# Attention times V by full-array products over two heads, in a sliding-window attention with a mixture of adapters

## The chip, the cores and the metric

One NeuronCore of a Trainium2 chip runs the whole program. The metric is the device time of one execution in microseconds. The engines are called PE (matrix products; PEld is its loading of weights), DVE (VectorE), ACT (ScalarE), POOL (GpSimd) and SP (SyncE). Each of them works through its own instructions in order and waits on semaphores for the others. Loads of q, k and v are issued from POOL's queue, stores of the output and loads of the adapters' weights from SP's.

## What is computed

There are 8 batches of 8 heads, 576 positions and 64 elements per head, all in float32. Attention is limited to a window of 32 positions to each side. Its output, with the heads side by side, is the input x (4608 rows of 512) of a mixture of 8 adapters of rank 16, of which each row takes the best two.

```python
scores = scale * np.matmul(q, k.transpose(0, 1, 3, 2))
mask = np.abs(pos[:, None] - pos[None, :]) <= window          # window = 32
attn = softmax(np.where(mask, scores, -1e9))
x = np.matmul(attn, v)            # then (B, H, S, D) -> (B * S, H * D)
logits = x @ w_gate;  topk = the two largest;  w = softmax over these two
delta = sum over the two of w * ((x @ A[e]) @ B[e])
return x + delta
```

## The kernel before

The 64 heads are taken in pairs. A pair's keys are cut into 9 blocks of 64 positions, and a block together with the queries that its window reaches is a slot; 8 slots make a score tile T, of which there are 36. For four steps n in a batch b there is one product with V, numbered u = 4b + n, so 32 of them.

The order of the work is written out by hand, as the string ORDER (lines 51 to 101): a list of words such as `PV.2:2`, each of which calls the function of that name, with its numbers; what follows the colon is the bank of PSUM (0 to 2 for the wide tiles W, 3 and 4 for the narrow tiles T) or the engine (A for ACT, D for DVE, P for POOL). The program keeps that order on each engine and on each queue. The words, in the order in which data passes through them:

- LD (line 166) loads 128 rows of q or k, LV (line 178) a batch's v in rows of two positions. With each row of v the two positions lie side by side, so SV (line 185) moves every second one to 32 other partitions. LV and SV of v are numbered by the half o of the partitions; there are 17 LV and 32 SV, 29 of these on POOL and 3 on DVE. Five v tiles take turns (NV, line 41); Z1 (line 505) sets their column of ones once.
- TR (line 194) turns q or k by 16 transposes on PE, EQ and EK (lines 204 and 214) copy them out of PSUM.
- SM (line 226) puts the mask into a score tile, by four products that each use a quarter of the PE array (64 rows, 64 columns) and write 512 columns. SC (line 239) adds the scores in 16 quarter products, EX (line 244) takes the exponential into a tile PT, whose borders ZP (lines 508 and 509) has cleared once.
- PV (line 262) multiplies PT by v. Head one of the pair lies in partitions 0 to 63 and head two in 64 to 127, both of PT and of v. Each of 13 steps is a pair of products, one for each half of the rows of the array, that write 65 columns each (a sum and 64 outputs) into different banks. So a PV has 26 matmuls.
- MU (lines 275 and 280) divides by the sums into x, one reciprocal and one product of 640 columns on DVE.
- TX, XE, PZ (lines 307, 313, 323) turn x and multiply it by the adapters' A and the gate; G1a, G1b, GA and G2 (lines 349 to 375) make the gates on DVE and ACT; TZ and ZE turn the result.
- PD (lines 420 and 424) multiplies by B. Where OB, which brings the output out of PSUM, is on ACT (line 447), PE also adds x, by four more matmuls (line 424); where OB is on DVE (line 449), DVE adds x. ST (line 455) stores.
- WM (line 501) does products of zeros and CM, MM, MC (lines 476 to 494) make the mask.

Of the kernel before, what the change touches and what calls it, by code (L numbers as in the profile page):

```python
# [29 lines left out]
QW = NR * FT + 8  # L30
GS = 188
VD = D + 1
V0 = 8
VW = 136
GV = 66
NS = NP * NB
NEG = -30000.0
NU = B * NP
NV, NPT, NRAW, NX, NXT, NOB = 5, 6, 5, 3, 3, 12
NW, NT = 3, 2  # L40
LB = B - 1

# [6 lines left out]


ORDER = """
CI Z1.0 CQ LD.0.0 Z1.3 ZP.5 LD.0.1 ZP.2 LD.1.0 ZP.0 LV.0.1 ZP.4 LD.1.1 LD.2.0 TR.0.0:3 CM
TR.0.1:4 EQ.0:A LD.2.1 WM.2.4:0 EK.0:D LD.3.0 ZP.1 MM:4 MC Z1.1 SM.1:0 LV.1.1 TR.1.0:4 TR.1.1:3
LD.3.1 EQ.1:D SM.0:1 EK.1:A LD.4.0 Z1.2 ZP.3 TR.2.0:4 SM.2:2 EQ.2:D SC.0 SV.0.1.1:P TR.2.1:3
EX.0 Z1.4 WM.0.4:4 EK.2:D LV.0.0 SC.2 LD.4.1 SC.1 EX.2 SM.3:1 SC.3 TR.3.0:3 LD.5.0 EX.1
TR.3.1:4 EQ.3:A SM.4:0 EX.3 WM.1.4:3 SV.1.1.0:P EK.3:A LD.5.1 SC.4 LD.6.0 SM.5:1 SV.0.0.0:D EX.4
TR.4.0:4 PV.2:2 LV.1.0 EQ.4:A PV.3:0 SC.5 SV.0.0.1:P MU.3 EX.5 TR.4.1:4 MU.2 LV.2.1 PV.1:0
EK.4:A SV.1.1.1:P PV.0:1 MU.1 SM.7:2 LD.6.1 MU.0 SM.8:0 SC.8 SC.7 TR.5.1:4 LD.7.0 EX.7 TR.5.0:3
LD.7.1 EK.5:D SM.6:1 EQ.5:A SC.6 LD.8.0 WG LV.2.0 WA EX.8 TX.0.1:4 LD.8.1 SM.9:2 EX.6 TR.6.0:3
SV.1.0.0:P SV.1.0.1:D TX.0.0:0 EQ.6:A SC.9 XE.0.0:D PV.5:1 EX.9 SV.2.1.0:P MU.5 PV.4:0 MU.4  # L60
SV.2.1.1:P SM.10:2 TR.7.0:3 XE.0.1:D PV.6:1 LV.3.1 MU.6 TR.6.1:4 LD.9.0 TX.0.2:0 EK.6:A LD.9.1
XE.0.2:D SM.11:1 PV.7:0 EQ.7:A TR.7.1:4 MU.7 SC.10 TR.8.0:3 EX.10 EK.7:D SC.11 SM.12:0
SV.2.0.1:P EX.11 EQ.8:D TX.1.0:4 WD:D LD.10.0 SC.12 SM.13:1 WC:D EX.12 SC.13 LD.10.1 PV.8:2
SV.2.0.0:P TR.8.1:3 EX.13 XE.1.0:D PZ.0:0 MU.8 LD.11.0 EK.8:A TX.1.2:4 G1a.0 SM.14:1 XE.1.2:A
LV.3.0 PV.9:2 G1b.0 GA.0 TX.1.1:3 SV.3.1.0:P MU.9 SC.14 TR.9.0:4 EX.14 XE.1.1:D LV.4.1 PV.11:2
G2.0 EQ.9:A SV.3.1.1:P TR.9.1:3 TR.10.0:1 EK.9:A LD.11.1 MU.11 PV.10:0 TZ.0:4 LD.12.0 EQ.10:D
TR.10.1:3 ZE.0:A LV.4.0 SM.17:2 MU.10 SC.17 TR.11.0:4 LD.12.1 EX.17 PD.0.3:1 EQ.11:D PZ.1:0
EK.10:A OB.0.3:D TX.2.1:4 G1a.1 TX.2.2:3 SV.3.0.0:P XE.2.1:A TX.2.0:1 XE.2.2:D PD.0.1:2 XE.2.0:D
PD.0.0:3 LD.13.0 OB.0.1:A PD.0.4:4 PD.0.2:1 OB.0.0:A OB.0.4:D SM.18:2 OB.0.2:A LV.5.1 SC.18
G1b.1 TR.11.1:3 GA.1 ST.0.2.2 EX.18 SV.4.1.0:P PZ.2:1 G2.1 ST.0.1.1 EK.11:A SV.3.0.1:P SM.15:2  # L70
SC.15 G1a.2 TZ.1:4 EX.15 SV.4.1.1:P G1b.2 SM.16:0 SC.16 ZE.1:D TR.12.0:3 GA.2 EX.16 LD.13.1 G2.2
PV.12:2 TR.12.1:4 EQ.12:A LV.5.0 SM.19:0 SC.19 MU.12 EK.12:A PV.14:1 SV.4.0.1:P PD.1.3:3 MU.14
# [12 lines left out]
OB.3.4:D TX.5.2:4 TX.5.1:1 G1a.4 XE.5.2:A PD.3.1:3 G1b.4 GA.4 TX.5.0:0 OB.3.1:A XE.5.1:D
TR.17.0:4 XE.5.0:A TR.16.0:3 EQ.17:D SM.27:1 EQ.16:A SC.27 G2.4 PZ.5:0 EX.27 TR.16.1:3
SV.7.1.0:P G1a.5 PD.3.0:4 G1b.5 EK.16:A TZ.4:1 SM.29:2 ZE.4:D SC.29 GA.5 OB.3.0:D EX.29 SM.30:1
PD.4.2:3 G2.5 SC.30 OB.4.2:A SM.31:2 SC.31 EX.30 PD.4.4:4 PD.4.0:3 OB.4.4:D PV.26:0 OB.4.0:A
PV.24:1 ST.4.4.24 MU.26 EX.31 PD.4.3:4 ST.3.1.16 ST.3.0.15 TR.17.1:3 MU.24 ST.4.0.20 OB.4.3:A
SV.7.0.0:P PV.27:2 ST.3.4.19 EK.17:A ST.4.2.22 PV.25:0 MU.27 TZ.5:4 SV.7.0.1:P SM.33:1 ZE.5:A  # L90
SC.33 MU.25 SM.32:2 EX.33 SV.7.1.1:P SC.32 PD.4.1:4 SV.8.1.0:D PD.5.1:3 SM.35:0 EX.32 OB.4.1:D
SM.34:1 SC.35 SC.34 OB.5.1:D ST.4.1.21 TX.6.0:4 EX.35 ST.3.2.17 PV.28:2 XE.6.0:D TX.6.1:3 EX.34
MU.28 PV.30:0 TX.6.2:4 XE.6.1:A PV.31:1 MU.30 PV.29:2 XE.6.2:A PD.5.0:3 MA.31 PZ.6:0 OB.5.0:A
MU.29 ST.5.0.25 PD.5.2:3 ST.4.3.23 MB.31 TX.7.0:4 G1a.6 OB.5.2:A TX.7.4:1 TX.7.2:2 G1b.6 GA.6
ST.5.2.27 TX.7.1:3 XE.7.0:A XE.7.4:D XE.7.1:A G2.6 PD.5.3:4 PD.5.4:1 XE.7.2:A TX.7.3:3 XE.7.3:A
PZa.7:2 OB.5.4:A OB.5.3:D TZ.6:3 PZb.7 ZE.6:D ST.5.4.29 ST.5.1.26 G1a.7 PD.6.0:3 ST.5.3.28 G1b.7
GA.7 PD.6.1:4 OB.6.0:A PD.6.2:1 G2a.7 OB.6.1:A ST.6.0.30 PD.6.4:3 OB.6.2:A PX.7.2:0 ST.6.1.31
OB.6.4:A G2b.7 TZa.7:4 PX.7.4:1 ZEa.7:A TZb.7:2 ST.6.4.34 PX.7.3:3 ZEb.7:A ST.6.2.32 PB.7.2
PX.7.1:4 OB.7.2:A PB.7.3 PB.7.1 OB.7.3:D PX.7.0:2 OB.7.1:A PB.7.4 ST.7.2.99 PB.7.0 PD.6.3:0
OB.7.4:A OB.7.0:D ST.7.3.99 ST.7.1.99 OB.6.3:A ST.7.4.99 ST.7.0.99 ST.6.3.33  # L100
"""


# [1 line left out]
def kernel(  # L105
# [62 lines left out]
            f += n  # L168

    def LV(b, o):
        h0 = 8 * b + (2, -2)[o]
        skip = 2 if h0 < 0 else 0
        n = min(h0 + 4, B * H) - h0 - skip
        src = v.rearrange("b h s d -> (b h) s d")[h0 + skip:h0 + skip + n]
        src = src.rearrange("n (a p two) d -> p (n a) (two d)", p=32, two=2)
        keep(nc.gpsimd.dma_start(  # L178
            out=vs[b % NV][64 * o:64 * o + 32, NB * skip:NB * (skip + n), V0:V0 + 2 * D], in_=src))


    def SV(b, o, h):
        d = vs[b % NV][:, NS // 2 * h:NS // 2 * h + NS // 2]
        p0 = 64 * o
        keep(copy_on("SV", b, o, h)(out=d[p0 + 32:p0 + 64, :, V0:V0 + D],  # L185
                                    in_=d[p0:p0 + 32, :, V0 + D:V0 + 2 * D]))


    def TR(t, w):
# [29 lines left out]

    QUARTERS = [(e, o, 64 * (o ^ e ^ 1)) for e in (0, 1) for o in (0, 1)]  # L220

    def SM(T):
        p = ps("SM", T).rearrange("p (i c) -> p i c", c=128)
        for e, o, r0 in QUARTERS:
            c0 = 64 * o
            keep(nc.tensor.matmul(  # L226
                out=p[r0:r0 + 64, 4 * e:4 * e + 4], lhsT=twice[c0:c0 + 64, 0:64],
                rhs=bcast(maskK[c0:c0 + 64], 1, 4), start=True, stop=False,
                tile_position=(c0, r0)))


    def SC(T):
# [17 lines left out]
    def PV(u):  # L250
        b, n = divmod(u, NP)
        po = ps("PV", u)
        for g in range(NG):
            ops = [(a, off) for a, off in ((2 * g - 1, 128), (2 * g, 64), (2 * g + 1, 0))
                   if 0 <= a < NB]
            for i, (a, off) in enumerate(ops):
                T, sl = divmod(NB * (2 * b + n % 2) + a, TB // 2)
                sl += TB // 2 * (n // 2)
                for o in (0, 1):
                    r = slice(64 * o, 64 * o + 64)  # L260
                    c0 = 512 * (o ^ (n < 2)) + GV * g
                    keep(nc.tensor.matmul(  # L262
                        out=po[:, c0:c0 + VD], lhsT=PTs[T % NPT][r, sl, off:off + 128],
                        rhs=vs[(b + (o and n // 2)) % NV][r, NB * (n ^ 2) + a, V0 - 1:V0 + D], start=(i == 0),
                        stop=(i == len(ops) - 1), tile_position=(64 * o, 0)))

    rcs = {}

    def sums(u):
        p = ps("PV", u).rearrange("p (h c) -> p h c", h=2)[:, :, 0:GV * NG]  # L270
        return p.rearrange("p h (g c) -> p g h c", c=GV)

    def recip(u):
        rcs[u] = small.tile([128, NG, 2], F32, tag="rc", name="rc")
        keep(nc.vector.reciprocal(out=rcs[u], in_=sums(u)[:, :, :, 0]))  # L275

    def mult(u, g0, g1):
        b, n = divmod(u, NP)
        xg = xs[b % NX].rearrange("p g (h n d) -> p g h n d", h=2, n=NP)
        keep(nc.vector.tensor_tensor(out=xg[:, g0:g1, :, n], in0=sums(u)[:, g0:g1, :, 1:VD],  # L280
                                     in1=bcast(rcs[u][:, g0:g1], 3, D), op=ALU.mult))

    def MU(u):
        recip(u)
# [217 lines left out]
                                  start=True, stop=True))  # L502

    def Z1(i):
        keep(nc.vector.memset(vs[i][:, :, V0 - 1:V0], 1.0))

    def ZP(i):
        keep(nc.vector.memset(PTs[i][:, :, 0:64], 0.0))
# [62 lines left out]
```

## Time and profile before

| | |
|---|---|
| three timed runs, us | 144.29, 144.80, 145.91 (median 144.8) |
| the profiled execution, us | 143.44, of which the span of its instructions is 141.6 |
| granted PE clock, mean | 0.964 |
| loads and stores | 28.85 MB read, 9.44 MB written |
| POOL's last load of v issued at, us | 83.2 |
| POOL's DMA issues of q, k and v | 24, 24 and 17 |

In the page, a group's row gives busy time, the mean of one in ns, then the idle time of the engine just before them and what ended it. In the windows view each row is a stretch of the span, with busy time and the number of instructions of each engine, the granted clock, the DMA share and GB/s. In the chain of waits, which follows the work that ended last back to the start, each row is a start, a duration and what filled it; "issue" is time in which an engine waited for nothing that the profile shows.

### The profile page before, as it was taken

Reading aid. Unit: us, or ns where it says so; the run is one execution under the profiler, and the core shown is the slowest. Engines: PE = TensorE matmul, PEld = TensorE weight load, DVE = VectorE, ACT = ScalarE, POOL = GpSimd, SP = SyncE. Lnnn points to the kernel's source line nnn. Section 1 sums busy time; section 2 is a strip of 40 time slices with the busy share of each in tenths; the row PEclk is TensorE's granted clock in tenths of the full one; section 3 lists DMA queues with packets and bytes.
Section 4 is the critical chain, followed back from the end, with each engine's and each line's share of the span. In section 5 each row is a group of like instructions: output and inputs, shape, how many; then the busy total and the mean of one; then the engine's idle time right before and its main releaser. Section 6 shows DMA issues by size and latency. Waiting matters only on the chain.

```text
span 141.6 us, 5983 instructions
## 1 busy us (share of the span) xinstructions
PE 113.2 (80%) x2637; PEld 85.5 (60%) x2637; DVE 96.5 (68%) x235; ACT 86.8 (61%) x116; POOL 78.7 (56%) x103
## 2 busy tenths in 40 slices
PE   0389977729595995899875999859999998999950
PEld 0237636627473784797753477647887775878830
DVE  7165306550856869977984599898889798997430
ACT  3113789175253748379871568575878889565850
POOL 7999879998099999999995773630000000000000
PEclk9999999995999599999998699999999999999999
DMA  0999999999999999999999399291660095153885
GB/s 0 188 195 199 199 191 203 184 203 184 224 199 202 187 192 172 176 147 174 192 226 189 50 155 233 71 304 49 227 192 0 5 283 197 47 199 110 282 315 172
DMA packets 35288, 24.50 MB, mean 173 GB/s; under 512 B 21312, under 2 KB 30528, under 8 KB 35264
## 3 DMA queue, kind: packets, MB, share of 16 engines
q0 software_dynamic: 28688, 14.16, 76.1%
q1 hardware_dynamic: 6576, 9.98, 21.5%
q8 instruction: 20, 0.33, 1.0%
q14 instruction: 4, 0.03, 0.1%
HBM read 28.85 MB, written 9.44 MB: 270 GB/s over the span
## 4 chain that ended last, share of the span: by engine, by line
PE 60%; DVE 17%; issue 10%; ACT 5%; DMA 3%; POOL 1%; DVEq 0%; POOLq 0%; ACTq 0%
PE W L262 9%; PE T L194 9%; PE W L226 7%; PE T L420 6%; PE W L239 6%; PE T L424 5%; PE W L323 5%; PE T L307 4%; DMA l<-in_k_dram 3%; DVE zs L375 3%; PE W L307 3%; ACT PT L244 2%; PE W L424 2%; DVE gate L367 2%; DVE x L280 2%
## 5 line engine op out<-in xcount | busy, mean ns | idle before, releaser
L244 ACT ACTIVATE PT<-W 128x1024 f16<-128x1024 f32 x36 | 36.3, 1027 | 16.0 <-PE W L239 12.7
L185 POOL COPY v<-v 32x1152 f16<-32x1152 f16 x29 | 33.5, 1160 | 13.0 <-DMA v<-in_v_dram 12.3
L194 PE MATMUL T<-ident,l 128*64 128x128 f16 x528 | 22.9, 235 | 10.1 <-DMA l<-in_q_dram 5.6
L194 PEld LDWEIGHTS <-l 128*64 128x64 f16 x576 | 19.3, 118 | 16.9 <-issue 8.3
L280 DVE TENSOR_TENSOR x<-W,rc 128x640 f16<-128x640 f32 (+2 forms) x33 | 26.5, 804 | 1.1
L262 PE MATMUL W<-v,PT 64*128 64x65 f16 x832 | 18.1, 193 | 4.8 <-issue 3.7
L214 ACT COPY kR<-T 128x1024 f16<-128x1024 f16 x14 | 14.2, 1016 | 9.4 <-PE T L194 9.3
L226 PE MATMUL W<-maskK,twice 64*64 64x512 f16 x144 | 16.1, 433 | 3.2 <-DVE zs L375 1.7
L262 PEld LDWEIGHTS <-PT 64*128 64x128 f16 x832 | 14.8, 96 | 6.2 <-issue 4.0
L239 PE MATMUL W<-qR,kR 64*64 64x128 f16 x576 | 15.8, 231 | 3.0 <-issue 2.5
L239 PEld LDWEIGHTS <-kR 64*64 64x64 f16 x576 | 12.4, 114 | 7.8 <-issue 5.1
L166 POOL DMA_DIRECT2D l<-in_q_dram x24 | 15.8, 661 | 0.9 <-DMA l<-in_q_dram 0.5
L166 POOL DMA_DIRECT2D l<-in_k_dram x24 | 15.6, 652 | 0.0
L204 ACT COPY qR<-T 128x1024 f16<-128x1024 f16 x10 | 10.2, 1015 | 5.8 <-PE T L194 5.8
L178 POOL DMA_DIRECT2D v<-in_v_dram x17 | 13.7, 806 | 0.0
L275 DVE RECIPROCAL rc<-W 128x10 f32<-128x10 f32 x32 | 6.9, 216 | 8.6 <-PE W L262 8.6
L447 ACT COPY ob<-T 128x512 f32<-128x512 f32 x14 | 8.2, 588 | 6.6 <-PE T L424 4.7
L424 PEld LDWEIGHTS <-xT 128*128 128x128 f16 x96 | 10.1, 121 | 3.2
L420 PE MATMUL T<-B_sb,zT 128*128 128x512 f16 x30 | 11.6, 410 | 0.4 <-ACT xT L313 0.2
L307 PEld LDWEIGHTS <-x 128*128 128x128 f16 x160 | 10.7, 118 | 1.4 <-issue 0.4
L323 PE MATMUL W<-WA_sb,xT 128*128 128x136 f16 x160 | 11.0, 223 | 0.0
L449 DVE TENSOR_TENSOR ob<-T,x 128x512 f32<-128x512 f32 x14 | 9.4, 685 | 2.0 <-PE T L420 1.8
(76 smaller groups left out, 148.3 us busy)
## 6 DMA issues: line engine op xcount, KB each, us to landing
out_dram<-ob SPq DMA_DIRECT2D x24, 256.0 KB, 2.8
v<-in_v_dram POOLq DMA_DIRECT2D x15, 288.0 KB, 7.6
l<-in_q_dram POOLq DMA_DIRECT2D x12, 256.0 KB, 6.5
l<-in_k_dram POOLq DMA_DIRECT2D x12, 256.0 KB, 7.1
out_dram<-ob SPq DMA_DIRECT2D x16, 192.0 KB, 2.7
l<-in_q_dram POOLq DMA_DIRECT2D x4, 192.0 KB, 6.7
l<-in_k_dram POOLq DMA_DIRECT2D x4, 192.0 KB, 5.7
l<-in_q_dram POOLq DMA_DIRECT2D x4, 128.0 KB, 7.4
```

The lines of the kernel that those rows point to most:

```text
L166: keep(nc.gpsimd.dma_start(out=raw[w][t % NRAW][f - FT * t:f - FT * t + n], in_=src[f - NF * b:f - NF * b + n]))
L185: keep(copy_on("SV", b, o, h)(out=d[p0 + 32:p0 + 64, :, V0:V0 + D], in_=d[p0:p0 + 32, :, V0 + D:V0 + 2 * D]))
L194: keep(nc.tensor.matmul(out=tp[64 * o:64 * o + 64, FT * slot:FT * slot + FT], lhsT=raw[w][t % NRAW][:, o, D * j:D * j + D], rhs=ident, is_ ...
L226: keep(nc.tensor.matmul(out=p[r0:r0 + 64, 4 * e:4 * e + 4], lhsT=twice[c0:c0 + 64, 0:64], rhs=bcast(maskK[c0:c0 + 64], 1, 4), start=True, ...
L239: keep(nc.tensor.matmul(out=p[r0:r0 + 64, 4 * e + i], lhsT=kR[r, a], rhs=qR[r, :, 8 * a:8 * a + 16], start=False, stop=(i == TB // 2 - 1), ...
L244: keep(nc.scalar.activation(out=PTs[T % NPT][:, :, 64:192].rearrange("p i (f j) -> p i f j", j=J), in_=ps("SM", T).rearrange("p (i j f) -> ...
L262: keep(nc.tensor.matmul(out=po[:, c0:c0 + VD], lhsT=PTs[T % NPT][r, sl, off:off + 128], rhs=vs[(b + (o and n // 2)) % NV][r, NB * (n ^ 2) ...
L280: keep(nc.vector.tensor_tensor(out=xg[:, g0:g1, :, n], in0=sums(u)[:, g0:g1, :, 1:VD], in1=bcast(rcs[u][:, g0:g1], 3, D), op=ALU.mult))
L307: keep(nc.tensor.matmul(out=tp[:, c0:c0 + 128], lhsT=fourth(xs[b % NX][:, g], c), rhs=ident, is_transpose=True, start=True, stop=True))
L323: keep(nc.tensor.matmul(out=pz(b)[:, GS * g:GS * g + ER + E], lhsT=xTs[b % NXT][:, g, c, :], rhs=WA_sb[:, c, :], start=(c == 0), stop=(c = ...
L420: keep(nc.tensor.matmul(out=pd, lhsT=zTs[b % 2][:, g], rhs=B_sb, **kw))
L424: keep(nc.tensor.matmul(out=fourth(pd, c), lhsT=xTs[b % NXT][:, g, c], rhs=ident, start=(first and c == 0), stop=(not first and c == 3)))
```

## The change

Five things are changed together.

1. PV no longer uses two half arrays. The v tile gets 194 columns instead of 136, so that each partition has room for both heads: partitions 0 to 63 hold head one in columns 0 to 64 (its ones first) and zeros in columns 129 to 193, partitions 64 to 127 hold head two in columns 129 to 193 (its ones last) and zeros in columns 0 to 64. A step of PV is one product with all 128 rows and 130 columns, 13 instead of 26 in a PV.
2. The zeros are written once, by the new word ZV, eight times 64 partitions of 36 x 65 elements, six on DVE and two on ACT. There are four v tiles instead of five. Z1 sets its ones in two pieces.
3. LV takes three loads for a batch instead of two that straddle batches (24 instead of 17, the same bytes), and v starts at an odd element of the tile. Of the 32 SV, 19 are on POOL and 13 on DVE.
4. MU takes the two heads in two products of 320 columns each where they have to be swapped (n of 0 and 1).
5. SM's mask is two products of half the rows and all columns, instead of four quarters.

ORDER is new as a whole. On PE it holds the same 233 steps. OB is on DVE 22 times instead of 18 (on ACT 18 instead of 22), and WD and WC, which convert the adapters' weights, are on ACT instead of DVE. One group of zero products (WM.2.4) stands at the end of PE's list instead of near the start.

```diff
-V0 = 8
-VW = 136
-GV = 66
+VW = 3 * D + 2
+V1 = VW - VD
+GV = 171
-NV, NPT, NRAW, NX, NXT, NOB = 5, 6, 5, 3, 3, 12
+NV, NPT, NRAW, NX, NXT, NOB = 4, 6, 5, 3, 3, 12
...
+    def LV(b, i):
+        h0, n, s0 = ((2, 4, 0), (6, 2, 0), (0, 2, 2))[i]
+        p0, c0 = (96, VD) if i else (0, 1)
+        src = v[b, h0:h0 + n].rearrange("n (a p two) d -> p (n a) (two d)", p=32, two=2)
         keep(nc.gpsimd.dma_start(
+            out=vs[b % NV][p0:p0 + 32, NB * s0:NB * (s0 + n), c0:c0 + 2 * D], in_=src))
...
     def SM(T):
         p = ps("SM", T).rearrange("p (i c) -> p i c", c=128)
-        for e, o, r0 in QUARTERS:
-            c0 = 64 * o
-            keep(nc.tensor.matmul(
-                out=p[r0:r0 + 64, 4 * e:4 * e + 4], lhsT=twice[c0:c0 + 64, 0:64],
-                rhs=bcast(maskK[c0:c0 + 64], 1, 4), start=True, stop=False,
-                tile_position=(c0, r0)))
+        for h in (0, 1):
+            r = slice(64 * h, 64 * h + 64)
+            keep(nc.tensor.matmul(out=p[:, 4 * h:4 * h + 4], lhsT=twice[r], rhs=bcast(maskK[r], 1, 4),
+                                  start=True, stop=False, tile_position=(64 * h, 0)))
...
-                for o in (0, 1):
-                    r = slice(64 * o, 64 * o + 64)
-                    c0 = 512 * (o ^ (n < 2)) + GV * g
-                    keep(nc.tensor.matmul(
-                        out=po[:, c0:c0 + VD], lhsT=PTs[T % NPT][r, sl, off:off + 128],
-                        rhs=vs[(b + (o and n // 2)) % NV][r, NB * (n ^ 2) + a, V0 - 1:V0 + D], start=(i == 0),
-                        stop=(i == len(ops) - 1), tile_position=(64 * o, 0)))
+                vv = vs[b % NV][:, NB * (n ^ 2) + a, 0:VD]
+                vv = dataclasses.replace(vv, ap=[list(vv.ap[0]), [V1, 2], [1, VD]])
+                keep(nc.tensor.matmul(
+                    out=po[:, GV * g:GV * g + 2 * VD], lhsT=PTs[T % NPT][:, sl, off:off + 128],
+                    rhs=vv, start=(i == 0), stop=(i == len(ops) - 1)))
...
+        U = sums(u, g0, g1)[:, :, 1:1 + 2 * D].rearrange("p g (h d) -> p g h d", h=2)
+        if n < 2:
+            for h in (0, 1):
+                keep(nc.vector.tensor_tensor(
+                    out=xg[:, g0:g1, 1 - h, n], in0=U[:, :, h],
+                    in1=bcast(rcs[u][:, g0:g1, h], 2, D), op=ALU.mult))
...
+    def ZV(i, o):
+        d = vs[i][64:128, :, 0:VD] if o else vs[i][0:64, :, V1:VW]
+        if where["ZV", i, o] == "A":
+            keep(nc.scalar.copy(out=d, in_=bcast(zero[64 * o:64 * o + 64, 0:VD], 1, NS)))
+        else:
+            keep(nc.vector.memset(d, 0.0))
```

129 lines of the change are left out of this document (63 added, 66 removed).

## The prediction

> **What bounds the kernel now.** I read the page first: busy times, slices, shares of the chain.
>
> ```profile
> PE 113.2 (80%) x2637; PEld 85.5 (60%) x2637; DVE 96.5 (68%) x235; ACT 86.8 (61%) x116; POOL 78.7 (56%) x103
> ...
> PEclk9999999995999599999998699999999999999999
> DMA  0999999999999999999999399291660095153885
> ...
> PE 60%; DVE 17%; issue 10%; ACT 5%; DMA 3%; POOL 1%; DVEq 0%; POOLq 0%; ACTq 0%
> ```
>
> PE carries 60% of the chain, and another 10% (14 us) is "issue". The DMA engines are full until about 78 us, yet DMA has only 3% of the chain: loads run ahead. So the question is what PE does all day, and what stops it. The view of PE's waits answers the second half (total, times, longest):
>
> ```profile
> PE W L262 <- issue: 3.7, 3, 2.0
> PE T L194 <- issue: 2.9, 2, 1.6
> PE W L239 <- issue: 2.5, 1, 2.5
> PE W L226 <- DVE zs L375: 1.7, 1, 1.7
> PE W L194 <- issue: 1.4, 1, 1.4
> ```
>
> Seven stops with no visible cause hold 10.5 us, on three unrelated lines; waits for other engines are small beside them. I then cut windows from the end of one stop to the end of the next. Columns: stretch, length, busy us and count for PE, PEld, DVE, ACT, POOL, then granted clock, DMA share, GB/s.
>
> ```profile
> 25.24:31.70 6.46, 3.52 (x128) 2.72 (x128) 4.12 (x9) 2.99 (x4) 6.36 (x9) 1.00 1.50 195
> 31.70:39.01 7.31, 5.79 (x127) 4.18 (x127) 3.16 (x6) 3.06 (x3) 3.27 (x5) 0.77 1.38 204
> 39.01:45.05 6.04, 4.14 (x128) 3.22 (x127) 3.68 (x7) 2.95 (x3) 6.00 (x8) 1.00 1.36 201
> 56.62:75.88 19.26, 15.91 (x382) 12.75 (x383) 15.09 (x39) 12.95 (x17) 19.09 (x23) 1.00 1.33 183
> 75.88:119.93 44.05, 41.01 (x1020) 30.48 (x1020) 37.88 (x84) 32.62 (x43) 9.94 (x11) 0.96 0.64 147
> 32.50:35.80 3.30, 3.30 (x51) 2.20 (x50) 0.46 (x1) 1.66 (x2) 2.44 (x4) 0.50 1.43 178
> 46.10:49.50 3.40, 3.40 (x80) 2.69 (x80) 3.04 (x10) 2.73 (x3) 3.40 (x5) 0.50 1.68 187
> 76.90:80.10 3.20, 3.20 (x52) 1.40 (x46) 2.36 (x5) 1.43 (x3) 1.27 (x2) 0.50 0.73 116
> 0.00:21.70 21.70, 14.23 (x262) 8.69 (x263) 8.94 (x27) 9.78 (x11) 19.18 (x34) 1.00 1.13 163
> ```
>
> The stops stand 128 matmuls and 128 weight loads apart, or a multiple of it (383 is three times, 1020 eight times, give or take a lost record). So instructions come to PE in blocks of 256, and while DMA is full a block needs 6.0 to 7.3 us from the end of one stop to the end of the next. PE runs its 256 in 3.5 to 4.1 us in two of these windows and then stands. The three rows at clock 0.50 follow the long stops before 31.70, 45.05 and 75.88 within 1.1 us: a stop also costs a stretch of half clock.
>
> So PE bounds the kernel almost from the start, partly by its own work, partly by the number of its instructions. The change moves these two against each other.
>
> **PE's own work.** The chain gives the pace of products, where PE waits for nothing:
>
> ```profile
> 21.77 0.93 PE W L262 x52
> ...
> 101.01 0.51 PE W L262 x26
> 101.52 0.32 PE T L420
> 101.84 1.18 PE W L323 x20
> ...
> 111.97 0.44 PE T L424 x4
> 112.41 0.91 PE W L262 x52
> ```
>
> A PV after other work takes 0.51, a second right behind it 0.91 - 0.51 = 0.40 (31 ns for a pair of 65 columns: the halves run side by side). After the change a step is one full-array matmul of 130 columns. The nearest row is L323's, full array and 136 columns: 1.18 / 20 = 59 ns. Scaled by columns it is 56.4; I take 57, bounds 56 and 59. A PV is then 13 x 57 = 0.74 us, 0.34 more; 32 of them: **+10.9** (bounds +10.5 and +11.8). The zeros are paid in full.
>
> The 0.11 between 0.51 and 0.40 is the price of changing how the array is divided. Counted in the two orders, such changes go from 124 to 119: **-0.5**.
>
> OB moves to DVE four times, and with it PE's four matmuls of 0.44 (L424) go: **-1.8**. SM halves its matmuls; its 512 columns pass in the same time if the two halves run side by side, as PV's did: 0. If they didn't, it would be 512 columns at 57 / 130 ns each, 0.22 us, times 36, +8; PV's 31 ns per pair speaks against it. PE's work: **+8.6**.
>
> **The start.** DVE gets six clears of 36 x 65 = 2340 elements, and all stand before the first PV. Rows by shape:
>
> ```profile
> L280 DVE TENSOR_TENSOR x<-W,rc 128x640 f16<-128x640 f32 x31 | 25.6, 825 | 1.1
> L449 DVE TENSOR_TENSOR ob<-T,x 128x512 f32<-128x512 f32 x14 | 9.4, 685 | 2.0 <-PE T L420 1.8
> ...
> L214 DVE COPY kR<-T 128x1024 f16<-128x1024 f16 x4 | 4.9, 1222 | 5.0 <-PE T L194 5.0
> L204 DVE COPY qR<-T 128x1024 f16<-128x1024 f16 x5 | 3.5, 693 | 3.5 <-PE T L194 3.4
> ...
> L185 DVE COPY v<-v 32x1152 f16<-32x1152 f16 x3 | 1.8, 589 | 5.2 <-DMA v<-in_v_dram 5.1
> L508 DVE MEMSET PT<- 128x256 uint32 x6 | 1.6, 272 | 0.0
> ...
> L505 DVE MEMSET v<- 128x36 f16 x5 | 0.4, 88 | 0.4
> L280 DVE TENSOR_TENSOR x<-W,rc 128x256 f16<-128x256 f32 x1 | 0.4, 415 | 0.0
> ```
>
> A clear of 256 words takes 272 ns, 1.06 each, so 2340 take 2.49 us; two f16 to a step would halve it to 1.24, and L505's rate (88 / 36) would make 5.7. Its 88 ns are mostly a fixed part, so I take 2.45. The Trainium skill, "VectorE: DVE Perf Modes", section "Zero memsets can be issued as uint32 (trn2)", says that a memset takes one cycle per element whatever the type, and that only a whole number of 4-byte words can be issued as uint32; rows of 65 f16 are none. By its 0.96 GHz that is an estimated 2.44 us; no run here shows it yet.
>
> DVE's list before the first PV: 6 x 2.45 clears, 8 clears of PT (2.2), three EQ (2.1), two EK (2.4), two SV (1.2), 1.5 of small ones: 24.1 us, from 0.9 on, with about half a us of waits. The first PV starts at some 25.5 where it began at 21.77. In between stand EQ.0, EK.0, EQ.2 and EQ.3, each behind clears, and behind them PE's SC.0 to SC.5 and ACT's EX. PE has as much work ahead of it as before, so **+4.0** (bounds 0, where later slack takes it up, and +6). The window to 21.7 shows the cover that is gone: DVE was busy only 8.94 us of it.
>
> **The instruction blocks.** PE's list falls by 416 PV and 72 SM matmuls, 16 more with OB, each with its load: 2637 to 2133, -19%. The same steps fill blocks less often. The window from 39.01 holds two PV and one SM: after the change it is 128 - 28 = 100 matmuls, and it runs 4.14 + 2 x 0.34 = 4.8 us; for 128 that is 6.2. Small waits on other engines bring it to about 6.4, against 6.0 to 7.3 until the next block is there. Some ten blocks fall into the time when DMA is full; I leave 0.25 us at each. The stops were 10.5, start to start 11.5 (a matmul's row outlasts its pace by 0.15): **-9.0** (bounds -11.5 and 0). The three half-clock stretches, at most 1.7 each by their length, cost an estimated 3.9; I leave 0.6: **-3.3** (bounds -3.9 and 0).
>
> The Trainium skill, "Runtime: NRT & Kernel Launch", section "Instruction fetch mechanics", agrees on 256 instructions a block, but has the cost of crossing one mostly hidden. The windows here show it open. By its rule fewer instructions gain nothing; that is the last rival.
>
> **What is covered.** MU in halves: (415 + 64/384 x 410) x 2 = 967 against 825 ns, 16 times, 2.3 us of DVE; four OB (2.7) and eight later SV (4.7 at most) come on top, WC and WD leave: about 8 us, on a DVE that was busy 88 of the 115 us after 21.7 (96.5 less 8.94). If that cover fails, it shows as PE waiting for W banks: 0 to +3, taken as 0. Ten SV less and seven LV more on POOL: it was busy 9.94 of the 44 us after 75.88, and loads have 3% of the chain. v at an odd element: no row prices it; a slower load hides in the same lead. LV on four tiles waits for an older PV, with LD queued behind on POOL; the lead covers that as well.
>
> **Sum.** 8.6 + 4.0 - 9.0 - 3.3 = +0.3 on 143.44 (span 141.6 and 1.8 around it), 143.7. The profiled run was 1.4 under the median, so on the median 144.8 + 0.3 = **145.1**.
>
> **Rivals.**
> 1. *The blocks still come late* (slower). Place: PE between 25 and 80 us. If each of ten blocks takes 7.3, as the second window's, against 6.4 of running, 9 us of stops stay instead of 2.5, and the half clock with them: 145.1 + 6.5 + 3.3 = 155; half of it gives 150. It decides once a block runs shorter than it takes to come. For: 7.3 was seen. Against: that window had a half-clock stretch in it. With it goes PE waiting on a fuller DVE, +3.
> 2. *The start costs little and the stops vanish* (faster). PE's first stops fall before 32 us, when it would now be held by DVE anyway; then 2.5 + 0.6 go, and 2 of the 4.0 are made up: 140.0. For: DMA keeps its lead. Against: PE is the bound to the end, so a late start stays late.
> 3. *Fewer instructions gain nothing* (slower), as the rule above has it: 145.1 + 9.0 + 3.3 = 157.4. The equal distance of seven stops speaks against it.
>
> **Numbers.** Forecast 0.44 (142 to 148), rival 1 0.25, rival 2 0.27, rival 3 0.04. One per cent, 1.45 us, is what a measurement of this kernel can tell from no change. The forecast splits into 0.10 faster, 0.21 same, 0.13 slower; rival 2 adds 0.26 faster and 0.01 same, rivals 1 and 3 0.29 slower. The range 139.5 to 152 leaves out the lower tail of rival 2 and the upper half of rivals 1 and 3.
>
> **What would show it.** PV at 57 ns a matmul and 0.74 each; clears of 2.45 us and a first PV near 25.5; stops 128 matmuls apart, together under 3 us; at most one half-clock row. The sum is wrong if PE waits for DVE by more than 5 us, if the mask's halves take turns, or if loads of v become what PE waits for.

## The result, and the profile after

The changed kernel takes 170.84 us (median of four runs, 170.51 to 173.99) beside 144.55 us for the kernel before: 1.190 times as long, 95% interval 1.173 to 1.208. The profiled execution took 170.74 us, with a span of 168.8. (Here and below the kernel before was timed anew beside each set of runs, with medians of 139.96 to 144.55 us; a ratio is taken within its set and leaves disturbed runs out while a median does not, so the two can differ a little.) The prediction of 145.1 us, with a range of 139.5 to 152, was wrong by 26 us.

The page of the changed kernel, with the rows that answer to those shown of before:

```profile
PE 128.6 (76%) x2133; PEld 97.6 (58%) x2133; DVE 112.1 (66%) x272; ACT 91.3 (54%) x116; POOL 72.0 (43%) x100
...
PEclk9999987999755697899999975997599999999998
DMA  1999999999999999999999999993100062392884
...
q0 software_dynamic: 28800, 14.16, 117.7%
q8 instruction: 16, 0.26, 0.8%
...
PE 46%; DMA 21%; DVE 20%; issue 7%; POOL 2%; SPq 1%; DVEq 0%
DMA v<-in_v_dram 16%; PE W L259 13%; DVE v L516 7%; PE T L193 5%; DMA out_dram<-ob 5%; PE W L237 5%; PE T L423 4%; PE T L310 4%; PE W L226 4%; PE T L427 3%; PE W L326 2%; DVE qR L203 2%; DVE kR L213 1%; PE W L310 1%; PE W L427 1%
...
v<-in_v_dram POOLq DMA_DIRECT2D x16, 144.0 KB, 12.3
v<-in_v_dram POOLq DMA_DIRECT2D x8, 288.0 KB, 11.2
```

The same three DMA rows of the kernel before:

```profile
q0 software_dynamic: 28688, 14.16, 76.1%
...
q8 instruction: 20, 0.33, 1.0%
...
v<-in_v_dram POOLq DMA_DIRECT2D x15, 288.0 KB, 7.6
```

q0 is the queue of the loads of q, k and v. It moves the same 14.16 MB, but its packets now take 117.7% of what 16 engines have in the span instead of 76.1%, and the span itself is longer: 117.7% of 168.8 us is 199 us per engine against 108. (It can pass 100% because packets overlap: in this trace up to 62 packets of v are under way at once on the 16 engines.) DMA is full for 26 slices of 4.2 us instead of 21 of 3.5, and the chain of waits, which had 3% of DMA, has 16% of loads of v alone. Two pieces of that chain, start and length in us:

```profile
37.28 15.46 DMA v<-in_v_dram
59.63 10.73 DMA v<-in_v_dram
```

What PE waits for no longer says "issue" seven times. It names engines that had to wait for v first (POOL's SV, and DVE's MU at the end of the first of the two pieces), and others, such as DVE's OB, which waits for the store of an output buffer:

```profile
PE T L490 <- POOL mask L484: 5.5, 1, 5.5
PE T L310 <- DVE x L283: 5.2, 1, 5.2
PE W L326 <- ACT WA_sb L539: 3.4, 1, 3.4
PE T L423 <- DVE ob L452: 3.3, 1, 3.3
PE W L237 <- issue: 3.2, 1, 3.2
PE W L259 <- POOL v L184: 3.2, 2, 2.3
```

The packet records of the trace, grouped by size (a packet of 256 bytes is v, one of 1024 is q or k), with the mean duration in ns and the middle 80%:

```
                v: mean  10%  median  90%     q, k: mean
before             41     41     41    41         102
changed           104     41     94   187         133
```

Of the 18432 packets of v, 61% take more than 50 ns, where before it was 1%; the fastest tenth takes 41 ns as before. The mean of q and k rises by 30%. The clock row shows what follows on PE: stretches of half clock, 30.7 us of them between the first PV and the end, behind most of its longer waits.

**A measure for the rest.** I add up the prediction's prices of PE's steps in the order of its list (PV 0.39 before and 0.74 after, SM and SC 0.225, TR 0.45, and so on, 0.09 for each change of the array's division). What a step's start exceeds that sum by is PE's lag: time in which it stood, or ran at half clock. The table has it for the kernels told of below. It is read from one execution of each, and in the last three rows the prices are good to about 1 us, since they depend on which neighbouring steps count as a change of the division.

| kernel (profiled execution) | PE's prices | lag at first PV | at PV.8 | at PV.18 | at the last step | span |
|---|---|---|---|---|---|---|
| before | 98.9 | 11.2 | 23.2 | 31.5 | 37.6 | 141.6 |
| changed | 107.8 | 19.2 | 38.1 | 45.9 | 56.6 | 168.8 |
| before, v at an odd element (e1) | 98.9 | 16.8 | 29.1 | 45.5 | 53.7 | 157.7 |
| changed, v shifted to even elements (e2) | 107.8 | 17.8 | 22.6 | 26.7 | 35.3 | 147.4 |
| e2, clears as words (e5) | 107.8 | 12.6 | 23.9 | 28.6 | 34.8 | 148.3 |
| e2, copies on DVE and 16 buffers (e6) | 107.8 | 17.7 | 20.8 | 24.5 | 27.8 | 140.0 |
| e6 with paired products (e9) | 97.5 | 18.8 | 26.8 | 33.5 | 40.2 | 142.4 |
| e9 without clears (e10) | 97.5 | 12.3 | 21.3 | 30.0 | 36.4 | 138.6 |
| e6, paired from unit 20 on (e12) | 104.4 | 19.4 | 21.3 | 25.0 | 29.5 | 138.4 |

In the changed kernel the prices rise by 8.9 us, close to the forecast 8.6, and the lag by 19 where a fall was forecast. Between 123 us and the end it hardly grows, so PE then runs at its forecast pace; what was lost was lost before.

### The profile page after: what moved, and what is told of

It reads as the page before. It is cut to its first block, busy times and chain, and to the rows that moved or that the text cites. A ratio compares the mean times of both kernels' runs of the same rounds, so it can differ in the third digit from the quotient of the medians.

```text
span 168.8 us, 5039 instructions
## 1 busy us (share of the span) xinstructions
PE 128.6 (76%) x2133; PEld 97.6 (58%) x2133; DVE 112.1 (66%) x272; ACT 91.3 (54%) x116; POOL 72.0 (43%) x100
## 3 DMA queue, kind: packets, MB, share of 16 engines
q0 software_dynamic: 28800, 14.16, 117.7%
## 4 chain that ended last, share of the span: by engine, by line
PE 46%; DMA 21%; DVE 20%; issue 7%; POOL 2%; SPq 1%; DVEq 0%
DMA v<-in_v_dram 16%; PE W L259 13%; DVE v L516 7%; PE T L193 5%; DMA out_dram<-ob 5%; PE W L237 5%; PE T L423 4%; PE T L310 4%; PE W L226 4%; PE T L427 3%; PE W L326 2%; DVE qR L203 2%; DVE kR L213 1%; PE W L310 1%; PE W L427 1%
## 5 line engine op out<-in xcount | busy, mean ns | idle before, releaser
L242 ACT ACTIVATE PT<-W 128x1024 f16<-128x1024 f32 x36 | 36.0, 1024 | 18.0 <-PE W L237 17.1
L259 PE MATMUL W<-v,PT 128*128 128x130 f16 x416 | 31.0, 230 | 4.5 <-POOL v L184 3.2
L259 PEld LDWEIGHTS <-PT 128*128 128x128 f16 x416 | 27.1, 102 | 7.4 <-issue 4.7
L184 POOL COPY v<-v 32x1152 f16<-32x1152 f16 x19 | 22.2, 1175 | 12.0 <-DMA v<-in_v_dram 11.7
L177 POOL DMA_DIRECT2D v<-in_v_dram x24 | 17.6, 735 | 13.5 <-DMA v<-in_v_dram 4.7
L193 PE MATMUL T<-ident,l 128*64 128x128 f16 x496 | 22.1, 245 | 0.1
L237 PEld LDWEIGHTS <-kR 64*64 64x64 f16 x576 | 10.9, 120 | 18.0 <-issue 16.8
L213 ACT COPY kR<-T 128x1024 f16<-128x1024 f16 x14 | 14.1, 1014 | 10.6 <-PE T L193 10.5
L452 DVE TENSOR_TENSOR ob<-T,x 128x512 f32<-128x512 f32 x19 | 12.8, 687 | 10.6 <-PE T L423 7.1
L226 PE MATMUL W<-maskK,twice 64*128 64x512 f16 x72 | 14.3, 428 | 6.6 <-DVE twice L495 2.9
L310 PE MATMUL T<-ident,x 128*128 128x128 f16 x124 | 10.7, 232 | 5.9 <-DVE x L283 5.2
L279 DVE TENSOR_TENSOR x<-W,rc 128x320 f16<-128x320 f32 x32 | 14.2, 486 | 0.6
L516 DVE MEMSET v<- 64x2340 f16 x6 | 12.0, 2008 | 2.9 <-issue 2.9
L283 DVE TENSOR_TENSOR x<-W,rc 128x640 f16<-128x640 f32 (+2 forms) x17 | 13.3, 785 | 0.6
## 6 DMA issues: line engine op xcount, KB each, us to landing
v<-in_v_dram POOLq DMA_DIRECT2D x16, 144.0 KB, 12.3
v<-in_v_dram POOLq DMA_DIRECT2D x8, 288.0 KB, 11.2
```

What stands on the lines that cost most here:

```text
L177: keep(nc.gpsimd.dma_start(out=vs[b % NV][p0:p0 + 32, NB * s0:NB * (s0 + n), c0:c0 + 2 * D], in_=src))
L184: keep(copy_on("SV", b, o, h)(out=d[p:p + 32, :, c0:c0 + D], in_=d[p0:p0 + 32, :, VD:VD + D]))
L193: keep(nc.tensor.matmul(out=tp[64 * o:64 * o + 64, FT * slot:FT * slot + FT], lhsT=raw[w][t % NRAW][:, o, D * j:D * j + D], rhs=ident, is_ ...
L213: keep(copy_on("EK", t)(out=kR[:, a0:a0 + BT].rearrange("p a (r f j) -> p a r f j", r=2, j=4), in_=kt))
L226: keep(nc.tensor.matmul(out=p[:, 4 * h:4 * h + 4], lhsT=twice[r], rhs=bcast(maskK[r], 1, 4), start=True, stop=False, tile_position=(64 * h ...
L237: keep(nc.tensor.matmul(out=p[r0:r0 + 64, 4 * e + i], lhsT=kR[r, a], rhs=qR[r, :, 8 * a:8 * a + 16], start=False, stop=(i == TB // 2 - 1), ...
```

## The experiments

### Where v lands (e1 to e4)

The theory: v now starts at element 1 or 65 of its row of 2-byte elements, so each packet of 256 bytes starts and ends in the middle of a 4-byte word, and that makes it slow. Rivals were the other things that changed around the loads: a row of 388 bytes instead of 272, three loads a batch, four tiles, and the clears.

```diff
# e1_before_odd, on the kernel before
-V0 = 8
+V0 = 7
```

> The kernel before with one number changed: v starts at element 7 of a row of the v tile instead of 8, so that each 256-byte packet of v lands at an odd 2-byte address; pitch, number of loads, tiles, order and everything else stay. Theory (the odd address makes a packet of v cost some 2.5 times as much): v packets near 100 ns as in the changed kernel against 41, queue share above 100%, DMA full past 100 us, and 155 to 170 us. Rivals (row pitch, three loads a batch, four tiles, or the clears at the start are the cause): v packets stay at 41 ns and the time within 1.5 us of 144.8.

Measured: 163.67 us beside 140.28, ratio 1.155 (1.131 to 1.180). One number, which moves no instruction, costs the kernel before 16% of its time. Rows of its page:

```profile
DMA  2999999999999999999999999599965009422885
...
q0 software_dynamic: 28688, 14.16, 121.4%
...
v<-in_v_dram POOLq DMA_DIRECT2D x15, 288.0 KB, 11.8
```

v's packets take 97 ns in the mean. The five v tiles, 17 loads, the pitch of 272 bytes and the old order are all still there, so nothing of what replaced them is needed for the loss. On PE much of it shows as stops of "issue", 19.5 us in ten instead of 10.5 in seven. For e2 the contents of each row are moved, and the row's pitch goes to 208 elements, which e3 tries alone:

```diff
# e2_after_aligned, on the changed kernel
-VW = 3 * D + 2
-V1 = VW - VD
+C0 = 7
+VW = 208
+V1 = C0 + 2 * D + 1
...
-        p0, c0 = (96, VD) if i else (0, 1)
+        p0, c0 = (96, C0 + VD) if i else (0, C0 + 1)
```

(with C0 added wherever a column of v is named).

> The changed kernel with the contents of every v row shifted by 7 elements and a row pitch of 208 elements: v now lands at elements 8, 72 and 136 (16-byte steps), the ones at 7 and 200, everything else as in the changed kernel. Theory (odd address): v packets back at 41 ns, queue share near 76%, and the time near what the prediction's other terms give, 140 to 152 us. Rival (three loads, four tiles): packets at 41 ns but still above 160 us. Rival (clears at the start): about 170 us less what DMA gives, first PV unchanged near 28.8 us and the lag kept to the end.

Measured: 150.37 us beside 140.28, ratio 1.082 (1.070 to 1.094). v's packets are back at 44 ns, and the span falls by 21.4 us, of which the table has 21.3 as lag. (The two spans are from different sets; within one set, e2's median lies 18.0 us under that of e3, told of next, which has v at an odd element.)

```profile
q0 software_dynamic: 28800, 14.16, 75.3%
...
v<-in_v_dram POOLq DMA_DIRECT2D x16, 144.0 KB, 7.9
v<-in_v_dram POOLq DMA_DIRECT2D x8, 288.0 KB, 7.9
```

e3 changes the pitch alone, e4 shifts by a single element (its rows then start at elements 2, 66 and 130):

```diff
# e3_after_pitch, on the changed kernel
-VW = 3 * D + 2
-V1 = VW - VD
+VW = 208
+V1 = 2 * D + 1
# e4_after_4B, on e2
-C0 = 7
-VW = 208
+C0 = 1
+VW = 196
```

> The changed kernel with the row pitch of the v tiles 208 elements (416 bytes) instead of 194 (388 bytes); v stays at an odd element. Theory (odd address): no change, 168 to 174 us, v packets near 104 ns. Rival (the row pitch, no multiple of 16 or 32 bytes): packets near 41 ns and 140 to 152 us, as the run with both changed.

> The changed kernel with the contents of every v row shifted by 1 element and a pitch of 196: v lands at elements 2, 66 and 130, so at a multiple of 4 bytes but not of 16. If what counts is a whole 4-byte word, v packets are at 41 ns and the time equals the run shifted by 7. If it is 16 or 32 bytes, packets stay near 100 ns and the time near 170 us; in between, the price grows with the bytes that do not fill a line.

Measured: e3 168.37 us, ratio 1.202 (1.178 to 1.227), v's packets at 99 ns: a wider row with v still at an odd element changes nothing. e4 148.97 us, ratio 1.057 (1.034 to 1.080), packets at 42 ns: a shift by a single element is enough, so here a whole number of 4-byte words is what counts, not 16 or 32 bytes. The row of v's queue, first of e3, then of e4:

```profile
q0 software_dynamic: 28800, 14.16, 114.4%
```

```profile
q0 software_dynamic: 28800, 14.16, 73.1%
```

The four runs settle the main cause. They leave 6 to 8%, which the prediction's sum does not have either.

### What is left once v is even (e5 to e8)

In e2 PE's lag jumps at two places, which its list of waits names:

```profile
PE T L424 <- DVE ob L453: 3.9, 1, 3.9
PE W L260 <- POOL v L185: 2.9, 1, 2.9
```

The chain of waits around the second of these lines, which comes first in time:

```profile
48.29 6.58 DMA v<-in_v_dram
54.87 0.28 issue
55.15 0.59 POOL l L169
55.74 1.16 POOL v L185
...
56.95 1.22 PE W L260 x13
```

A copy that PV.8 needs (SV.2, on POOL) stands in POOL's list behind issues of loads, and PE waits 2.9 us. From 47.1 to 55.7 us POOL issues eleven loads, at 0.5 to 0.7 us each; the chain leads on to an earlier load of v, for whose landing the last of them waits, but only 0.3 us. The other stop, from the same view at another time:

```profile
86.56 8.00 DMA out_dram<-ob
...
95.01 0.70 DVE ob L453
```

OB.2.2 needs an output buffer whose store, held back to a late place in SP's list, is still under way: 12 buffers take turns, and PE waits 3.9 us behind DVE. Around the end of each stop a stretch of half clock begins (in the windows view, columns as before):

```profile
57.40:60.81 3.41, 3.41 (x42) 3.04 (x39) 1.11 (x3) 0.96 (x2) 3.37 (x5) 0.50 1.46 184
94.95:101.77 6.82, 6.02 (x86) 4.56 (x86) 4.66 (x13) 3.11 (x4) 0.00 (x0) 0.50 0.12 42
```

```diff
# e5_clears_as_words, on e2
-        d = vs[i][64:128, :, C0:C0 + VD] if o else vs[i][0:64, :, V1:V1 + VD]
+        d = vs[i][64:128, :, C0 - 1:C0 + VD] if o else vs[i][0:64, :, V1:V1 + VD + 1]
...
-            keep(nc.vector.memset(d, 0.0))
+            keep(nc.vector.memset(d.bitcast(mybir.dt.uint32), 0))
# e6_copies_and_buffers, on e2
-NV, NPT, NRAW, NX, NXT, NOB = 4, 6, 5, 3, 3, 12
+NV, NPT, NRAW, NX, NXT, NOB = 4, 6, 5, 3, 3, 16
...
-G2.1 PD.0.4:3 EX.14 SV.2.0.1:P TR.9.0:4 OB.0.4:A LV.4.0 SM.12:2 SV.2.1.1:D EX.10 SM.13:1 SC.12
-EQ.9:D LD.14.0 SC.13 PD.0.3:3 EX.12 SV.2.1.0:P SV.2.0.0:D PV.8:0 OB.0.3:D EX.13 TR.9.1:4 MU.8
+G2.1 PD.0.4:3 EX.14 SV.2.0.1:D TR.9.0:4 OB.0.4:A LV.4.0 SM.12:2 SV.2.1.1:D EX.10 SM.13:1 SC.12
+EQ.9:D LD.14.0 SC.13 PD.0.3:3 EX.12 SV.2.1.0:D SV.2.0.0:D PV.8:0 OB.0.3:D EX.13 TR.9.1:4 MU.8
```

> The shifted kernel (v at elements 8, 72, 136) with each clear of v widened from 65 to 66 columns and issued as 33 words of 32 bits a row. Theory (DVE's clears hold the start): a clear falls from 2.0 us to about 1.1, six of them give 5 us, the first PV comes at 22.5 to 25 us instead of 27.4, and the kernel ends 2 to 5 us earlier, 145 to 148, since PE is the bound behind it. Rival (the start is covered, loads set the pace until 55 us): the first PV comes earlier but the end moves by less than 1 us, because the wait for v before PV.8 grows by what was gained.

Measured: 149.80 us beside 140.70, ratio 1.068 (1.047 to 1.088). A clear falls from 2008 to 1048 ns, and the first PV comes at 22.1 us instead of 27.4. In the profiled execution, of 150.10 us where the four took 147.70 to 150.10, almost nothing of these 5.3 us reaches the end (lag 34.8 against 35.3), because PE then waits for v:

```profile
PE W L260 <- POOL v L185: 7.1, 2, 5.8
...
PE W L260 <- DVE v L510: 2.6, 1, 2.6
```

This is the rival's mechanism. The ratios, 1.068 here and 1.082 for e2, differ by some 2 us with intervals that overlap, so a small gain, between the rival's and the theory's, isn't ruled out.

> The shifted kernel with the two POOL copies of v in front of PV.8 put on DVE, and 16 output buffers instead of 12. Theory (PE's two middle stops come from POOL's queue and from an output buffer not yet stored): the stop of 2.9 us at PV.8 and that of 3.9 us at PD.2.2 go, with them the half-clock stretches that follow (0.50 near 57 and 95 us), and the time is 142 to 147. Rival (the stops are only a sign of full DMA): PE waits there or a few steps later for DMA instead, and the time stays within 1.5 us of 150.

Measured: 142.48 us beside 140.70, ratio 1.020 (1.005 to 1.034). Both stops are gone, and the two stretches of half clock with them, though one of 6.8 us now stands around the first PV, where e2 had none; the span falls by 7.4 us, more than the 6.8 of the two stops. Beside the three long waits of the start (for the mask, for the tile `twice` that is multiplied with it, and for qR), PE's list holds only small ones:

```profile
PE W L227 <- DVE zs L379: 1.2, 1, 1.2
PE T L398 <- DVE ob L453: 1.0, 1, 1.0
PE W L238 <- DVE kR L214: 0.9, 1, 0.9
PE W L260 <- issue: 0.6, 1, 0.6
```

> The shifted kernel with the word clears, the two copies on DVE and 16 output buffers together. If the gains add: 138 to 143 us, beside 140 to 145 of the kernel before. If loads are the bound until the middle, no better than the better of the two parts.

Measured for e7, both edits together: 144.05 us beside 140.70, ratio 1.030 (1.016 to 1.045). The first PV comes at 21.0 us and the last step at the same place as in e6, within 0.6 us: an early start is lost again to waits for v (5.6 us at L260), so the gains do not add.

```diff
# e8_mask_quarters, on e2: SM as in the kernel before
+        for e, o, r0 in QUARTERS:
+            c0 = 64 * o
+            keep(nc.tensor.matmul(out=p[r0:r0 + 64, 4 * e:4 * e + 4], lhsT=twice[c0:c0 + 64, 0:64],
+                rhs=bcast(maskK[c0:c0 + 64], 1, 4), start=True, stop=False, tile_position=(c0, r0)))
```

> The shifted kernel with the mask made by four quarter-array products per SM again instead of two half-array ones: 72 instructions pairs more and nothing else. If the two halves run side by side (the prediction's 0): PE's work is the same, the time within 1.5 us of 150. If they take turns: quarters are 0.2 us shorter each, up to 8 us faster. If fewer instructions are what keeps PE from standing at block boundaries: quarters bring 1 to 3 us of stops back.

Measured: 147.28 us (144.38 to 150.13) beside 140.70, ratio 1.045 (1.023 to 1.067). The chain gives the pace of the mask in both forms, first e2 with halves:

```profile
63.51 0.32 PE W L227 x2
64.50 0.54 PE W L227 x4
```

then e8 with quarters:

```profile
62.50 0.34 PE W L227 x4
63.38 0.56 PE W L227 x8
```

A second mask right behind a first takes 0.54 - 0.32 = 0.22 us either way: the halves do run side by side. The 3 us by which e8's median lies under e2's don't come from the mask's pace; in its profiled execution the waits for SV and for the output buffer are 2.4 and 1.8 us instead of 2.9 and 3.9, and no half clock follows them. Why these waits are shorter stays open. Stops of "issue" are 1.3 us in all, where PE's list of e2 has none: the low end of what the third theory gave for 72 pairs of instructions more, and lost in the scatter of the time.

### Do fewer instructions gain anything? (e9 to e12)

e6 is a kernel in which the forecast of the stops can be tried in both directions, since DMA is full for longer than before (25 slices of 3.5 us, 21 in the kernel before) and v's packets are fast. e9 takes only PV back to pairs, with MU reading the sums where the pairs put them:

```diff
# e9_paired_clears, on e6
-                vv = vs[b % NV][:, NB * (n ^ 2) + a, C0:C0 + VD]
-                vv = dataclasses.replace(vv, ap=[list(vv.ap[0]), [V1 - C0, 2], [1, VD]])
-                keep(nc.tensor.matmul(
-                    out=po[:, GV * g:GV * g + 2 * VD], lhsT=PTs[T % NPT][:, sl, off:off + 128],
-                    rhs=vv, start=(i == 0), stop=(i == len(ops) - 1)))
+                for o, c in ((0, C0), (1, V1)):
+                    r = slice(64 * o, 64 * o + 64)
+                    keep(nc.tensor.matmul(
+                        out=po[:, 512 * o + GV * g:512 * o + GV * g + VD],
+                        lhsT=PTs[T % NPT][r, sl, off:off + 128],
+                        rhs=vs[b % NV][r, NB * (n ^ 2) + a, c:c + VD], start=(i == 0),
+                        stop=(i == len(ops) - 1), tile_position=(64 * o, 0)))
```

> The kernel of e6_copies_and_buffers (shifted v, two copies on DVE, 16 output buffers) with attention times V as pairs of half-array products again, each into its own bank, in place of one full-array product over both heads; order, loads, clears, mask and copies stay. PE's work falls by the prediction's 10.9 us, its matmuls rise by 416 with as many weight loads. Theory (PE's work is the bound behind the loads, and 416 more instruction pairs bring stops at block boundaries back): stops with no visible cause return, 3 to 8 us of them, and the time is 136 to 142. Rival (fewer instructions never mattered): no stops return and the time is e6 less 8 to 11, 131 to 134. Rival (loads are the bound to the end): within 1.5 us of e6, 142.

Measured: 146.62 us beside 141.90, ratio 1.040 (1.021 to 1.060). The interval overlaps with e6's, so that e9 is slower than e6 is not shown; that some 10 us less of PE's work gained nothing is. The page and the waits of e9:

```profile
PE 113.0 (79%) x2549; PEld 83.4 (59%) x2549; DVE 112.0 (79%) x274; ACT 90.3 (63%) x116; POOL 69.5 (49%) x98
...
PEclk9999998699997799999999995999999999999996
...
q8 instruction: 20, 0.33, 0.9%
```

```profile
PE W L260 <- issue: 5.9, 5, 3.0
```

Against e6 the lag grows by as much as PE's work falls, and 2 us more (12.4 by the table). Stops of "issue" are 5.9 us instead of 0.6, and behind the first PV PE runs at half clock for 6.8 us instead of 4.5. The remaining part, about half, is spread over small waits that I have not taken apart. It need not be a price of instructions: where another engine sets the pace, less work on PE only makes PE's waits longer, and DVE has 38% of e9's chain of waits, 16% of e6's. So 416 pairs of instructions bring back the stops that the first theory gave (3 to 8 us), while the time misses all three theories.

The trace also has what the stops wait for. q8, "instruction", moves packets of 16384 bytes: 20 for the 2637 matmuls and as many loads of weights of the kernel before, 16 for 2133, 20 again for e9's 2549, so about one for each block of 256. All seven stops of "issue" in the kernel before end 1.35 to 1.60 us after such a packet has ended, as do the five of e9 (1.38 to 1.59) and, within 1.2 to 1.8 us, the ten of e1. In the kernel before a packet takes 0.9 to 1.6 us throughout; what comes late is its start. Counted from PE's first matmul of the block ahead, the nine packets between 22 and 75 us, while DMA is full, start 1.4 to 4.9 us later, and those after 78 us at most 2.5 us later.

e10 is e9 without the eight words ZV.

> The same as the run with paired products, and the clears of the other head's columns, which paired products do not read, left out. The start gets earlier by 5 to 6 us. Theory (loads set the pace until about 75 us, so an early start is lost again): less than 2 us faster than with the clears. Rival (the start counts in full): 4 to 6 us faster.

Measured: 141.82 us beside 141.90, ratio 1.019 (1.003 to 1.035): 4.8 us under e9 in the median, 3.8 in the span, some 3 by the two ratios, whose intervals overlap. So of the start's 6.4 us half or more reaches the end, between the theory and the rival or as the rival had it, while with full-array products (e5, e7) little or nothing did.

```diff
# e11_before_halves, on the kernel before
-NV, NPT, NRAW, NX, NXT, NOB = 5, 6, 5, 3, 3, 12
+NV, NPT, NRAW, NX, NXT, NOB = 5, 6, 5, 3, 3, 16
```

SM is that of the change, with two products.

> The kernel before with two changes: the mask by two half-array products per SM in place of four, so 72 instruction pairs fewer, and 16 output buffers instead of 12. If instruction pairs cost stops: 144 instructions less are 0.56 of a block of 256, so some 0.5 to 1 us less, within the scatter of the kernel before. If the halves take turns: up to 8 us slower. If the buffers matter there too: 1 to 4 us faster.

Measured: 141.50 us beside 141.90, ratio 1.001 (0.988 to 1.015): no difference that can be told from the scatter. Its profiled execution, of 137.18 us, has 6.9 us of "issue" stops and one stretch of half clock behind the first PV, where that of the kernel before, of 143.44, had 10.5 us and three: so much do single executions of nearly the same kernel differ. Halves that take turns, up to 8 us slower, are ruled out once more; whether the 72 pairs or the buffers bring a little stays open.

e12 uses each form where it costs least: full-array products while DMA is full, pairs afterwards.

```diff
# e12_mixed, on e6
+PAIRED = 20
...
+                if u >= PAIRED:
...
+                    continue
```

In place of the second line of dots stand the two products of e9, and MU reads the sums at the places of the form that the unit has.

> The kernel of e6_copies_and_buffers with both forms of the product: full-array products over both heads for units 0 to 19, as the change has them, and pairs of half-array products for units 20 to 31, which run when DMA is no longer full (from about 90 us on). Theory (while DMA is full the number of instructions sets the pace, afterwards PE's own work does): no stops come back, twelve units save 0.34 us each, 4.1 us, and the time is 136.5 to 139.5, 1 to 3% under the kernel before. Rival (stops come with the number of instructions wherever they stand): 156 pairs more bring 2 to 4 us of stops, and the time stays at 141 to 143. Rival (the end is set by something other than PE): no change against 142.5 either, with PE waiting for DVE or ACT in the last 30 us.

Measured: 139.92 us beside 139.96, ratio 1.005 (0.999 to 1.011): the lowest ratio of any form of the changed kernel, and no better than the kernel before, just above what the theory gave. The windows show where pairs pay. First e6, then e12 (the 6 us in which PV.20 to PV.23 run, and the 23 us with the other eight):

```profile
92.00:98.00 6.00, 5.78 (x124) 4.99 (x118) 5.76 (x14) 4.31 (x7) 0.93 (x1) 1.00 0.14 48
98.00:121.00 23.00, 23.00 (x400) 18.10 (x389) 19.80 (x53) 16.89 (x22) 0.00 (x0) 1.00 0.30 107
```

```profile
92.00:98.00 6.00, 5.11 (x165) 4.34 (x164) 5.70 (x15) 4.01 (x7) 1.14 (x1) 1.00 0.15 51
98.00:121.00 23.00, 22.92 (x546) 17.03 (x535) 21.11 (x57) 17.45 (x23) 0.00 (x0) 1.00 0.33 117
```

From PV.8 to PV.20 the two kernels run alike within 0.3 us. In the 6 us DVE is busy for 5.76 and 5.70: there DVE is as full as PE, and the first units in pairs gain nothing, since PE stands for what they save (busy 5.11 instead of 5.78). In the 23 us PE is busy throughout, so there a saving counts: e12 is 1.4 us ahead at PV.31 and 1.7 at the last step, of the 4.1 expected. Stops of "issue" stay at 0.5 us.

## Why the prediction was wrong

**The step that failed** is the sentence under "What is covered": "v at an odd element: no row prices it; a slower load hides in the same lead." The first half was true, and I then priced it at nothing instead of bounding it from both sides. The lead was there for loads that keep their speed. A load of v that takes 104 instead of 41 ns a packet adds 62 ns to 18432 packets, 72 us on each of 16 engines; q0 was at 76.1% with DMA full for 78 of 141.6 us, so no lead could hold that. The condition was named as the last of those that would make the sum wrong ("loads of v become what PE waits for"), with no chance in the cases. e1 and e2 measure it from both sides: 16% on the kernel before, and 21.4 us of the changed kernel's 27.2 us of longer span (18.0 by the medians of e3 and e2, within one set).

**A second, smaller one** stands beside it: "LV on four tiles waits for an older PV, with LD queued behind on POOL; the lead covers that as well." Not that wait, but POOL's list cost 2.9 us at PV.8, since a copy that PE needs stood behind eleven issues. The prediction had read POOL's slack from the 44 us after 75.88, while its own rows have POOL busy for 19.09 of the 19.26 us before that. And the new order of the stores was not looked at: OB.2.2 waited for a buffer, another 3.9 us. With the half clock behind them the two make 7.4 us (e6).

**PE's own work: +8.6, confirmed.** By the prediction's own prices the two orders differ by 8.9 us. The price that was new is measured, for the chain of the changed kernel has the new PV where PE waits for nothing:

```profile
147.34 0.77 PE W L259 x13
148.55 0.76 PE W L259 x13
```

0.76 against 0.74, which makes 0.6 us in 32 of them. The mask's halves run side by side, as forecast (e8).

**The start: +4.0, measured +7.1.** The sum for it gives 25.5 - 21.77 = 3.7, of which the prediction made 4.0. The clears take 2008 ns each, not 2450, and 1048 as 1188 words:

```profile
L516 DVE MEMSET v<- 64x2340 f16 x6 | 12.0, 2008 | 2.9 <-issue 2.9
```

The Trainium skill ("VectorE: DVE Perf Modes", section "Zero memsets can be issued as uint32 (trn2)") has one cycle per element, an estimated 2.44 us, above the row; that words halve a clear, as it says, is what e5 shows. The first PV comes at 28.8, not 25.5, though the clears are shorter than forecast: DVE stands before each of them for 0.4 to 0.6 us, 2.9 us in all as the row has it, and for another 2.6 us before EQ.3, for transposes that PE did late since it had waited for EQ.2. The forecast had half a us for all such waits. (PE's wait of 5.5 us for the mask costs nothing: it ends at 5.5 us, and in the kernel before PE waited for q until 5.6.) What the start is worth at the end is not one number: little or nothing with full-array products (e5, e7), some 3 to 4 us of 6.4 with pairs (e10).

**Instruction blocks and half clock: -9.0 and -3.3, the mechanism confirmed, the size only roughly.** Once v is even, stops of "issue" fall from 10.5 us to 0.6 (e6; none in e2's list). The half clock behind the first PV, 10.2 us before, is still 10.2 in e2, behind the two new stops, and 4.5 in e6. By the table, lag from the first PV to the end grows by 26.4 us in the kernel before and by 10.1 in e6, a gain of 16.3 where 12.3 were forecast; but e6 also has two more edits, and e11's execution, with 6.9 us of stops, shows that the number for the kernel before can be several us smaller. e9 runs the other way: 416 pairs of instructions more bring 5.3 us of stops back. The Trainium skill ("Runtime: NRT & Kernel Launch", section "Instruction fetch mechanics") has the crossing of a block mostly hidden; while DMA is full, the runs here speak against it, and rival 3 falls. In e12, with 156 pairs more when DMA is no longer full, it is hidden indeed. So the cause is the instruction count together with full DMA, as the prediction had it, and the packets of q8 show the link: a stop ends when a block that started late has landed.

**The sum.** In e6, where v lands on even elements and the two new stops are gone, the table gives 8.9 + 6.5 - 16.3 = -0.9 us of PE's time against the one profiled execution of the kernel before, a span of 140.0 against 141.6. Within e6's own set the kernel before ran faster than that, and e6 takes 1.020 times as long (1.005 to 1.034), some 3 us more. The forecast of +0.3 us lies between the two: its terms fit that kernel to a few us, partly because the start's 3 us too little and the gain's 4 us too little cancel. The kernel that was forecast had v's loads at an even element's price; the kernel of the change did not.

## What to carry to other kernels

When a tile's layout changes, look first at the byte address at which each DMA lands: an odd 2-byte element cost these loads more than everything else in the change together, and a shift by one element took it back. A price that no row shows is to be bounded by its worst case and carried as a rival; "hidden by the lead" holds only as long as the transfers keep their speed, and is to be checked against the share of time in which DMA is already full. In this kernel PE's instructions were worth counting as well as its columns while DMA was full; once it wasn't, only the columns counted, and only where no other engine was as full as PE (e12).

## What the runs showed of the hardware

A packet of v at an odd element is not slow by itself. Grouped by how many packets of v are under way on the 16 engines when it starts, its mean duration in the changed kernel is:

```
packets of v under way     2-3   8-11  16-19  24-27  28-31   32 and more
changed, ns                 44     59     80     59     61      147
e2 (even elements), ns      41     42     41     41     42       59
```

With few others it takes nearly the 41 ns of an aligned one; with 32 and more it takes 147. This is a correlation within these traces, and no run varied the number alone: packets that take longer also raise the number under way, so the table can't tell which of the two comes first, and what slows the packets stays open. These loads also convert from 4-byte to 2-byte elements on the way, and whether a plain copy would show the same wasn't tried.
